# An FFT convolution's start-up: order of the first loads, two weight jobs ahead, 20 fillers

## The chip, the cores and the metric

The kernel runs on one core of a Trainium2 chip. A core has a matrix engine (TensorE, PE in the profile; its weight loads are listed as PEld), a vector engine (VectorE, DVE), an activation engine (ScalarE, ACT), a general engine (GpSimd, POOL) and a sequencer that issues transfers (SyncE, SP). Transfers are carried by 16 DMA engines. The metric is device time in microseconds for one execution; the kernel before takes 270.54 us, the median of three runs (270.21 to 270.58).

## The reference

A 7x7 convolution over a 224 x 224 picture with 96 channels in and 96 out, computed through Fourier transforms, so that both picture directions wrap around:

```python
wp = jnp.pad(w, ((0, H - K), (0, W - K), (0, 0), (0, 0)))
Xf = rfft2(x.astype(float32), axes=(1, 2))          # x: 1 x 224 x 224 x 96, bf16
Wf = rfft2(wp.astype(float32), axes=(0, 1))         # w: 7 x 7 x 96 x 96, bf16
Yf = jnp.einsum('bhwi,hwio->bhwo', Xf, Wf)
y = irfft2(Yf, s=(H, W), axes=(1, 2)).astype(bfloat16)
```

Because of the wrap-around, the first output columns need the last six columns of the picture, and the first rows need its last six rows.

## The kernel before, in words

The kernel does not transform the whole picture. It cuts the height into 8 blocks of 28 rows (with 6 rows of overlap, 34 in all), transforms each block along the height with a small matrix `Fm` (17 complex frequencies, held as real numbers), convolves along the width directly with 7 taps at each frequency, and transforms back with a small matrix `Gm`. The width is cut into 7 tiles of 32 columns. Products with a complex number are done with three real ones, and pairs of neighbouring columns are combined so that fewer products are needed; the combined planes are called `J`, and DVE computes them from the transformed pixels `xf`.

The weights need a transform of their own. `w` is loaded into `wq`, and a matrix `Em`, which stands behind it in the same buffer, turns it into the 50 planes of `WF`. This is done in groups of frequencies (`PGRP`): `prep_jobs(0)` covers frequencies 0 and 1, `prep_jobs(1)` frequencies 2 to 4, and so on. A group has 12 jobs, each of four TensorE products into one PSUM bank and a cast of that bank into `WF`; groups after the first end with three more jobs, subtractions on DVE (`diff`, WF from WF), which need all casts of their group.

Casts out of PSUM go through `evac`. It keeps a running cost for DVE and ACT in `load` and gives each cast to the engine whose cost is lower, as the program is written out, not as it runs. Each engine then works strictly in the order of the program text. There are eight PSUM banks, taken in turn; a product waits until the bank it takes has been cast.

What concerns the start, in the order of the program:

- SP issues the loads, lines 178 to 189. First come the wrap-around pixels, that is the last six columns (`xh_bufs`, two halves of the height with two transfers each: 112 rows and 6 rows, 1152 bytes a row), then the first half of the first tile's pixels (`load_x(0, 0)`, 112 rows and 6 rows of 6144 bytes), then the weights in five chunks, each in two transfers (2 partitions and 96), then the second half of the first tile's pixels, which waits for the third chunk of weights.
- Each of SP's transfers uses one of eight completion counters in turn. A transfer waits, before it is issued, until the transfer eight places ahead of it has landed.
- TensorE runs products on zeros (`warm`, tile `wu`): 17 at the very start, and 22 (line 707) between the products of the first pixels and those of the weights. All products of the weights wait for all five chunks.
- TensorE then transforms the wrap-around pixels (`a_bank`), the first half's pixels in three parts by frequency (`f_jobs`), runs the 22 fillers, the 12 jobs of the first weight group (48 products, line 709), and the second half's first part (line 711, 32 products).
- DVE makes the first planes `J` (line 715, `jit(0, 0)`), while POOL is still computing the matrix `Gm` (`build_g`, line 290) from a long chain of small operations; ACT takes its sine (`g_fin`, line 717, tile `ct` in the profile) and POOL forms the product (`Gm`).
- Then come the rounds (`b_round`), one for each frequency. Round 0 computes products from `xf` into one bank (copied by ACT to `tt_`), then `mid` jobs, products from `J` into a second bank, the sum `yf` on DVE, and `end` jobs. The second weight group's jobs are spread over `mid` and `end` of round 0 by `pace` (lines 744 and 745): 8 of its 15 jobs in `mid`, 7 in `end`.

From the third tile on the same rounds go on, with the transform of the next tile and the inverse transform of the tile before filled in between.

Of the kernel before, what the change touches and what calls it, by code (L numbers as in the profile page):

```python
# [32 lines left out]
PGRP = ((0, 2), (2, 5), (5, 8), (8, 11), (11, 14), (14, 17))  # L33
# [18 lines left out]
def slot(s, part):  # L52
    return part if s == 0 else 2 + 3 * (s - 1) + part
# [3 lines left out]
def kernel(  # L57
# [7 lines left out]
    _, H, W, C = x.shape  # L65
# [40 lines left out]
    def bank():  # L106
        return pools["psb"].tile([128, 512], F32, name="pb")

    load = {"v": 0.0, "a": 0.0}
# [3 lines left out]
    def apart(key, zone, r):  # L113
        for z, q in parts.setdefault(key, []):
            if z != zone and q.engine != r.ins.engine:
                tc.declare_no_dep(r.ins, q, reason="disjoint parts of one tile")
        parts[key].append((zone, r.ins))
        return r

    def evac(out_ap, in_ap, n):  # L120
        if tail[0]:
            return tail_evac(out_ap, in_ap, n)
        cv, ca = 180 + 1.0 * n, 160 + 0.85 * n
        if load["v"] + cv <= load["a"] + ca:
            load["v"] += cv
            return VE.tensor_copy(out=out_ap, in_=in_ap)
        load["a"] += ca
        return SE.copy(out=out_ap, in_=in_ap)
# [35 lines left out]
    def load_rows(xb, jg, w0, npx):  # L164
        h0 = jg * HB - PAD
        n = npx * C

        def ld(p0, p1, hh):
            return dma(xb[p0:p1, 0:n], x[0, hh:hh + (p1 - p0), w0:w0 + npx, :].rearrange("h w c -> h (w c)"))
        return ld(PAD, R, h0 + PAD), ld(0, PAD, h0 % H)  # L170

    def xbuf(t, jg):
        return (xn_bufs if t else x0_bufs)[jg]

    def load_x(t, jg):
        return load_rows(xbuf(t, jg), jg, t * 2 * TW, 2 * TW)

    wsrc = w.rearrange("kh kw i o -> (kh kw) (i o)")
    for jg in range(2):
        load_rows(xh_bufs[jg], jg, W - PAD, PAD)  # L180
    load_x(0, 0)
    wcut = [WC * c // NWC // 128 * 128 for c in range(NWC)] + [WC]
    wdma = []
    for c0, c1 in zip(wcut, wcut[1:]):
# [10 lines left out]
    def warm(n):  # L195
        pwu = bank()
        for _ in range(n):
            TE.matmul(pwu[:].rearrange("p (a b) -> p a b", a=4), lhsT=wu[:, 0:128], rhs=wur, start=True, stop=True)
# [141 lines left out]
    def prep_jobs(gi):  # L340
        s0, s1 = PGRP[gi]
        ns = s1 - s0
        full = gi == 0
        ncol = (NSLOT_OF(s0, s1) if full else 2 * ns) * NTAP
        nb = C // NB
        hb = NB // 2
        assert NB * ncol <= 512 and C2 % hb == 0

        def mk_(ob):
            def f():  # L350
                pw = bank()
                pv_ = pw[:, 0:NB * ncol].rearrange("p (k h q) -> p k h q", h=2, q=ncol)
                ev = Em[:, :, slot(s0, 0):slot(s1 - 1, 2) + 1, :]
                ev = ev.rearrange("p h a t -> p h (a t)") if full else ev.rearrange("p h (s r) t -> p h s (r t)", r=3)[:, :, :, 0:2 * NTAP]
                for k in range(hb):
                    o = ob * hb + k
                    TE.matmul(pv_[:, k], lhsT=wqx[0:PW2, o:o + 127 * C + 1:C], rhs=ev, start=True, stop=True)
                pv_ = pv_[0:C]
                o0, o1 = ob * hb, (ob + 1) * hb
                wv = WF[0:C, slot(s0, 0):slot(s1 - 1, 2) + 1]  # L360
                if full:
                    wv = wv.rearrange("i a t (h o) -> i (a t) h o", h=2)
                    apart(("W", gi), ob, evac(wv[..., o0:o1], pv_.rearrange("i k h q -> i q h k"), NB * ncol))
                    return
                wv = wv.rearrange("i (s r) t (h o) -> i s (r t) h o", r=3, h=2)
                apart(("W", gi), ob, evac(wv[:, :, 0:2 * NTAP, :, o0:o1],
                      pv_.rearrange("i k h (s q) -> i s q h k", s=ns), NB * ncol))
            return f

        def diff(s):  # L370
            def f():
                load["v"] += 60 + C * NTAP / 1.92
                w0, w1, w2 = (WF[0:C, slot(s, r)].rearrange("i t o -> i (t o)") for r in range(3))
                VE.tensor_tensor(out=w2, in0=w0, in1=w1, op=ALU.subtract)
            return f
        return [mk_(ob) for ob in range(nb)] + ([] if full else [diff(s) for s in range(s0, s1) if s not in REAL])

    def NSLOT_OF(s0, s1):
        return slot(s1 - 1, 2) + 1 - slot(s0, 0)
# [324 lines left out]
    for p in range(3):  # L704
        for f in fj[p][0]:
            f()
    for n in (11, 11):
        warm(n)
    for f in prep_jobs(0):
        f()  # L710
    last = [f() for f in fj[0][1]]
    for jg in range(2):
        for d in load_x(1, jg):
            tc.add_manual_dep(d.ins, last[0].ins.name, SYNC, reason="second tile's pixels later")
# [26 lines left out]
    def add(a, b, jobs):  # L741
        qs.append([a, b, jobs, len(jobs)])

    for gi in range(1, len(PGRP)):
        add(2 * PGRP[gi - 1][0], 2 * PGRP[gi - 1][1] - (2 if gi == 1 else 1), prep_jobs(gi))
    for t in range(2):
        scr_tiles[t] = dr_pool.tile([TW, NJ, NS, 4 * C], BF16, name="scr")
    bursts = {}
# [163 lines left out]
```

## Time and profile before

| | |
|---|---|
| median of three runs | 270.54 us (270.21 to 270.58) |
| profiled execution | 270.74 us, span of its instructions 269.0 us |
| granted TensorE clock | 0.997 |
| busy: PE, PEld | 257.9 us, 237.1 us |
| busy: DVE, ACT, POOL | 214.3 us, 195.5 us, 99.4 us |
| chain that ended last | PE 64%, DMA 12%, DVE 11%, ACT 7% |

The profile is one execution. Its span runs from the first to the last instruction; the time of the execution has 1.74 us more around it. A row of the timeline gives start, duration, engine, operation, tiles written and read, the size, how many instructions the row holds, and in brackets how long the engine had been idle and what ended that. A row of the chain gives the start, the length and the work that all later work waited for. A row of the windows gives, for a stretch of time, the busy time of each engine and the number of its instructions, then the granted clock, the share of time that the 16 DMA engines were busy, and GB/s. All kernel lines are recorded as one line (L89), that of a helper, so rows are told apart by their tiles.

### The profile page before, as it was taken

To read this page: it belongs to the slowest core of one execution; us is meant where nothing else is said; L and a number is where in the kernel's file an instruction comes from. 1 tells how busy PE (TensorE), PEld (TensorE's weight loads), DVE (VectorE), ACT (ScalarE), POOL (GpSimd) and SP (SyncE) were. 2 spreads that over 40 slices of the span, in tenths; PEclk is the share of its full clock that TensorE was granted. 3 is DMA by queue.
4 is the path that set the end of the run, shared out by engine and by line. 5 is a ranking of instruction groups with operands and counts; after the bars stand their busy time and mean duration, and the time that the engine had idled before them with its cause. 6 is when DMAs were issued, how large, how long until landed. Compare 5 with 4: busy or idle time off the path is not lost.

```text
span 269.0 us, 12171 instructions
## 1 busy us (share of the span) xinstructions
PE 257.9 (96%) x5144; PEld 237.1 (88%) x5144; DVE 214.3 (80%) x457; ACT 195.5 (73%) x483; POOL 99.4 (37%) x156
## 2 busy tenths in 40 slices
PE   8899999999999999999999999999998999899993
PEld 3679999999998999999999998989997989779862
DVE  5649998889899788778787888777887889778724
ACT  5549988587974578988988789886986864467113
POOL 7782315363647435322322222234132242522100
PEclk9999999999999999999999999999999999999998
DMA  6948011811111597987976486989658834888866
GB/s 171 230 129 217 6 46 46 243 47 67 46 46 50 163 276 135 294 249 206 289 207 198 133 246 192 250 223 332 224 151 152 255 98 154 198 231 212 223 118 205
DMA packets 47014, 46.78 MB, mean 174 GB/s; under 512 B 35286, under 2 KB 37986, under 8 KB 46960
## 3 DMA queue, kind: packets, MB, share of 16 engines
q1 hardware_dynamic: 44672, 43.94, 59.2%
q10 hardware_dynamic: 2288, 2.06, 2.8%
q8 instruction: 40, 0.66, 1.1%
q14 instruction: 14, 0.11, 0.1%
HBM read 24.65 MB, written 21.33 MB: 171 GB/s over the span
## 4 chain that ended last, share of the span: by engine, by line
PE 64%; DMA 12%; DVE 11%; ACT 7%; issue 3%; SPq 2%; DVEq 0%; ACTq 0%
PE pb L89 64%; DMA tt<-scr 5%; DMA wq<-in_w_dram 5%; DVE J L89 4%; ACT WF L89 3%; ACT xf L89 2%; DVE v L89 2%; DVE WF L89 2%; SPq L89 2%; DMA xf<-scrb 2%; DVE u L89 1%; DMA scrb<-yf 1%; DVE yf L89 1%; DVE xf L89 0%; DVE tt L89 0%
## 5 line engine op out<-in xcount | busy, mean ns | idle before, releaser
L89 PE MATMUL pb<-WF,J 96*128 96x96 bf16 x2821 | 162.6, 206 | 1.1 <-DVE J L89 0.9
L89 PEld LDWEIGHTS <-J 96*128 96x128 bf16 x2821 | 138.0, 98 | 10.5 <-issue 2.2
L89 POOL TENSOR_TENSOR yf<-v,u 128x384 bf16<-128x384 f32 x79 | 81.4, 1042 | 147.3 <-issue 86.9
L89 ACT CAST xf<-pb 96x408 bf16<-96x408 f32 (+3 forms) x145 | 67.8, 490 | 8.9 <-PE pb L89 5.3
L89 PE MATMUL pb<-WF,xf 96*128 96x96 bf16 x952 | 59.9, 206 | 0.5 <-ACT xf L89 0.5
L89 DVE TENSOR_TENSOR J<-xf 96x1824 bf16<-96x1824 bf16 (+1 forms) x84 | 56.9, 716 | 0.1
L89 PEld LDWEIGHTS <-xf 96*128 96x128 bf16 x952 | 47.0, 98 | 0.7 <-ACT xf L89 0.6
L89 PE MATMUL pb<-Fm,xn 118*128 118x136 bf16 (+3 forms) x640 | 45.5, 199 | 0.2 <-DVE u L89 0.2
L89 PE MATMUL pb<-tt,Gm 102*84 102x384 bf16 (+1 forms) x132 | 32.7, 327 | 2.4 <-DMA tt<-scr 2.3
L89 ACT CAST WF<-pb 96x480 bf16<-96x480 f32 (+1 forms) x59 | 29.1, 577 | 5.3 <-PE pb L89 5.3
L89 PEld LDWEIGHTS <-xn 118*128 118x128 bf16 x640 | 30.3, 97 | 0.3 <-issue 0.3
L89 ACT CAST J<-pb 84x384 bf16<-84x384 f32 (+1 forms) x64 | 27.6, 488 | 2.3 <-PE pb L89 2.0
L89 ACT CAST yo<-pb 84x384 bf16<-84x384 f32 (+1 forms) x63 | 26.9, 482 | 2.7 <-PE pb L89 2.7
L89 DVE TENSOR_TENSOR J<-J 96x912 bf16<-96x912 bf16 (+2 forms) x42 | 24.2, 576 | 0.0
L89 PE MATMUL pb<-wq 98*128 98x120 bf16 (+1 forms) x288 | 21.3, 226 | 0.3 <-DMA wq<-in_w_dram 0.3
L89 PEld LDWEIGHTS <-wq 98*128 98x128 bf16 x288 | 19.5, 151 | 0.8 <-issue 0.8
L89 PE MATMUL pb<-wu 128*128 128x512 bf16 (+1 forms) x75 | 16.5, 382 | 1.1 <-DVE ct L89 1.1
L89 PEld LDWEIGHTS <-wu 128*128 128x128 bf16 (+1 forms) x75 | 8.8, 119 | 7.7 <-issue 2.4
L89 DVE TENSOR_TENSOR yf<-v,u 128x384 bf16<-128x384 f32 x26 | 14.9, 571 | 0.9
L89 PEld LDWEIGHTS <-Gm 102*84 102x84 bf16 (+1 forms) x132 | 11.0, 117 | 3.5 <-DMA tt<-scr 2.9
L89 ACT COPY xf<-xf 96x816 bf16<-96x816 bf16 (+3 forms) x20 | 11.3, 632 | 0.0
L89 DVE CAST WF<-pb 96x480 bf16<-96x480 f32 (+1 forms) x13 | 7.5, 611 | 4.7 <-PE pb L89 4.7
(386 smaller groups left out, 234.4 us busy)
## 6 DMA issues: line engine op xcount, KB each, us to landing
scr<-yf SPq DMA_DIRECT2D x30, 288.0 KB
xn<-in_x_dram SPq DMA_DIRECT2D x12, 672.0 KB
tt<-scr SPq DMA_DIRECT2D x24, 336.0 KB
out_dram<-yo SPq DMA_DIRECT2D x12, 252.0 KB
out_dram<-J SPq DMA_DIRECT2D x12, 252.0 KB
tt<-scr SPq DMA_DIRECT2D x6, 288.0 KB
WF<-in_x_dram SPq DMA_DIRECT2D x2, 672.0 KB
out_dram<-tt SPq DMA_DIRECT2D x8, 168.0 KB
```

Of the source, the lines that this page charges most:

```text
L89: r = fn(*a, **k)
```

## The change

Three edits, all in the start:

1. `load_x(0, 0)` is issued ahead of the wrap-around pixels instead of behind them. The ten weight transfers stay behind both.
2. The first two jobs of the second weight group are written out right behind the first tile's second half (after line 711), ahead of `jit(0, 0)`, of `g_fin` and of round 0. Before them `load["v"]` is raised by a million, so that both casts go to ACT; the costs are reset a few lines on, as before. The other 13 jobs of that group are spread over round 0: 7 in `mid`, 6 in `end`.
3. The fillers are 10 + 10 instead of 11 + 11.

```diff
     wsrc = w.rearrange("kh kw i o -> (kh kw) (i o)")
+    load_x(0, 0)
     for jg in range(2):
         load_rows(xh_bufs[jg], jg, W - PAD, PAD)
-    load_x(0, 0)
...
-    for n in (11, 11):
+    for n in (10, 10):
         warm(n)
     for f in prep_jobs(0):
         f()
     last = [f() for f in fj[0][1]]
+    early = prep_jobs(1)
+    load["v"] += 1e6
+    for _ in range(2):
+        early.pop(0)()
...
     for gi in range(1, len(PGRP)):
-        add(2 * PGRP[gi - 1][0], 2 * PGRP[gi - 1][1] - (2 if gi == 1 else 1), prep_jobs(gi))
+        add(2 * PGRP[gi - 1][0], 2 * PGRP[gi - 1][1] - (2 if gi == 1 else 1), prep_jobs(gi) if gi > 1 else early)
```

Since `evac` counts costs as the text is written out, some later casts change their engine too: two go from DVE to ACT and one from ACT to DVE in round 0, and 11 between 183 and 217 us of the profile before (six from ACT to DVE, five from DVE to ACT).

## The prediction

> **What bounds the kernel now.** I read the busy shares and slices first, then the chain of waits, then the timeline of each engine for the first 45 us, where all three parts of the change lie, and last the DMA share by window.
>
> ```profile
> PE 257.9 (96%) x5144; PEld 237.1 (88%) x5144; DVE 214.3 (80%) x457; ACT 195.5 (73%) x483; POOL 99.4 (37%) x156
> ```
>
> TensorE is the busiest engine, but that is a mean. The chain, followed from the start to 50 us, says what each stage waits for:
>
> ```profile
> 9.55 6.52 DMA wq<-in_w_dram
> 16.07 0.14 issue
> 16.21 0.69 PE pb L89 x8
> ...
> 19.68 1.03 ACT xf L89 x2
> ...
> 21.63 4.19 ACT WF L89 x9
> ...
> 33.36 0.32 ACT tt__905 L89
> ...
> 41.53 1.75 DVE J L89 x2
> 43.28 0.28 DVE u L89
> ```
>
> The weight transfer sets the end of the first 16 us. From 16.9 to 33.7 us the chain lies on ACT, from 33.8 to 43.6 on DVE, and only then on TensorE (products, 64% of the whole chain). So the stage that the change touches is bounded by transfers, then by ACT, and TensorE has room in it. The rows of that stage:
>
> ```profile
> 10.98 4.91 PE L89 MATMUL pb<-wu 128*128 128x512 bf16 x22
> 16.21 3.15 PE L89 MATMUL pb<-wq 98*128 98x100 bf16 x48 [0.32 <-DMA wq<-in_w_dram]
> 20.76 0.51 PE L89 MATMUL pb<-WF,xf 96*128 96x96 bf16 x8 [0.46 <-ACT xf L89]
> 19.63 1.07 ACT L89 CAST xf<-pb 96x512 bf16<-96x512 f32 x2
> 20.89 0.37 ACT L89 ACTIVATE ct<-ct,ct 102x84 f32<-102x84 f32 x1 [0.19 <-POOL ct L89]
> 21.31 0.32 ACT L89 COPY tt__556<-pb 128x192 f32<-128x192 f32 x1
> 21.57 4.25 ACT L89 CAST WF<-pb 96x480 bf16<-96x480 f32 x9
> 21.27 1.10 DVE L89 TENSOR_TENSOR J<-xf 96x1824 bf16<-96x1824 bf16 x1
> 20.50 0.36 POOL L89 TENSOR_TENSOR ct<-ct,ct 102x84 f32<-102x84 f32 x1
> 21.34 1.27 POOL L89 TENSOR_TENSOR Gm<-ct,ct 102x84 bf16<-102x84 f32 x1 [0.48 <-ACT ct L89]
> ```
>
> The reader is to see three things: the products of the weights start when the transfer lands; TensorE waits about half a microsecond at 20.2 for ACT; and ACT itself waits at 20.70 for POOL's chain of small operations (the inverse matrix), which ends at 20.86 whatever the other engines do.
>
> **The change part by part.** Call d the time by which the weight products start earlier than 16.21.
>
> *Pixels first.* SP issues six pixel transfers from 0.80 to 3.06, then ten of weights. Bytes and issues are the same; only the order differs. The share of the 16 DMA engines at the start:
>
> ```profile
> 1.80:2.50 0.70, 0.70 (x3) 0.30 (x2) 0.53 (x4) 0.69 (x3) 0.62 (x3) 1.00 0.75 191
> 2.50:3.50 1.00, 1.00 (x4) 0.30 (x2) 0.93 (x5) 1.00 (x1) 0.73 (x5) 1.00 0.72 158
> 3.50:4.50 1.00, 1.00 (x4) 0.36 (x3) 0.40 (x2) 0.98 (x2) 0.85 (x5) 1.00 0.88 195
> ```
>
> (The last two columns are DMA share and GB/s.) Unused: 0.25 x 0.70 + 0.28 x 1.00 + 0.12 x 1.00 = 0.58 us. From 4.5 to 13 us the share is 1.02 to 1.05, so nothing is lost later. Short wrap-around rows (1152 B) go out first, in four issues of about 0.38 us, and the DMA engines run dry between them. With the long rows (6144 B) first there is a queue from the first packet on, so up to 0.58 us of it comes back. The nearest rows bound it: above by 1.57 us, the time by which the long rows' issue moves (from 2.37 to 0.80, the fifth place to the first); below by a loss (second rival). I take 0.6, the idle time, since bytes and packets stay.
>
> Behind these issues stand the weights'. In the built program each of SP's transfers takes one of eight completion counters in turn and waits until the transfer eight before it has landed. So the second weight chunk waits for transfers one and two, now the long rows instead of the wrap-around rows. Today that chunk is issued at 4.15 to 5.20 and its slowest engine needs it at 9.53, when the first chunk has landed (the issue at 9.55 waits for just that). With the long rows landing some 1.5 us earlier than today (7.46 for the 112 rows, 8.15 for the six, when SP's issues at 7.48 and 8.17 are released), the issue comes at about 6.0 to 6.7, plus 1.0 us to the first packet (0.80 to 1.80 today) 7.7, against a need at about 8.9. It fits, by about 1.2 us. The second tile half's pixels (issued at 12.92, behind the third chunk) move with the weights. TensorE takes the wrap-around products first; they now land last, but POOL's padding at 7.46 to 7.77 holds the sixth of them in any case, so I cost that at nothing; without that cover it would be the lateness of the landing.
>
> *20 fillers.* 22 take 4.91 us, 0.22 each, so TensorE is free 0.44 earlier: the last product ends at 15.89 today, 15.45 then, which is 0.76 before 16.21 (0.9 if the next products enter the pipe before that end). Fillers do not bind at d = 0.6; they would if the weights came more than that earlier.
>
> *Two early jobs.* Eight products of 0.065 us (32 take 2.1) = 0.5 us move into TensorE's wait at 20.2, and their two casts go to ACT by force. TensorE is thus 0.5 us further on, but it is not the bound here: the next bank, ACT and DVE set the pace (gain 0 on the path; it shows as slack). SP's loads of the second tile (20.24) wait for a pixel cast that still precedes the early ones. What counts is ACT. Before: the last pixel cast starts 20.12, then ct at 20.89, the copy, nine weight casts (0.455 from start to start; the last starts at 25.21 and ends 25.82). After, from the pixel cast: 20.60 - d first early cast, 21.06 - d second, 21.51 - d ct, but not before 20.89; then copy after 0.27 (no wait for the products now), casts after 0.26 more, eight of them, the last ending at ct + 0.53 + 7 x 0.455 + 0.60 = ct + 4.32. DVE gets two of the twelve casts instead of three, so ACT does one more, 0.455, paid by its waits (0.19 for POOL, some 0.15 for the products) and by the room ahead of POOL. With d = 0.6, ct = 20.91 and the last cast ends at 25.23, 0.59 earlier; with larger d POOL's 20.86 holds it at 0.61. So **the gain is about d, and never over 0.61**.
>
> From 25.7 to 33.7 ACT runs back to back, DVE's weight differences wait for that last cast (25.85 after 25.82), and DVE waits 0.44 us for ACT at 33.77, then runs back to back to 43.55, where TensorE waits for it. So the shift is handed on to 43.6 in full. From there TensorE is the chain; all loads hang on work that shifts alike.
>
> *Evacuations that change engine later.* The planner's running costs shift, and 11 casts from 183 to 217 us change between ACT and DVE, six to DVE, five to ACT. At 183.4 DVE gets a pixel cast (0.35 from start to start); a product at 190.86 needs a bank that DVE's u frees at 190.69, 0.17 us of room, so 0.0 to 0.2 is lost there, and an extra cast at 201.4 falls into 0.9 us of idle DVE. Bounds: -0.2 to +0.4 in all; I take +0.1.
>
> Sum, against the profiled execution's 270.74 (span 269.0, 1.74 around it): -0.6 + 0.1 = -0.5, 270.24. That execution is 0.20 above the median of the three runs, so **270.05** in the median.
>
> **The rivals.**
>
> *POOL is blocked by DVE.* The same POOL shape, 102x84, takes 0.36 us at 20.50 and 1.27 at 21.34, the latter beside DVE's J operation, which runs 21.27 to 22.37: POOL ended 0.24 after it. J starts when the pixel casts end, 21.27 - d. If d is over 0.77, J begins before POOL's sum at 20.50; that sum then ends about 20.42 + 1.10 + 0.24 = 21.76 instead of 20.86; ACT's ct waits for it, the tt copy and eight casts are queued behind ct, DVE's weight differences wait for these casts, and the gain of 0.6 becomes a loss of 0.3: with the later casts 270.9. The Trainium skill, SBUF — State Buffer, section "Who interferes with whom", says that a tensor_tensor with both inputs in SBUF contends with GpSimd's reads, and that whichever is issued first holds the ports for the whole instruction. By that rule, too, an order with POOL first would only delay J, and the trace's 1.27 against 0.36 agrees. For it: the fillers let d reach 0.76 to 0.9. Against: the DMA's idle time gives 0.6. Chance 0.2.
>
> *The counters starve the DMA: slower.* If the long rows land no earlier than today (7.46, 8.15), the second chunk is issued at about 8.2 to 8.8 and its first packet comes at 9.2 to 9.8, at or after the need at 9.53; each later chunk is pushed likewise. From that point every microsecond counts in full: 0.3 to 0.8 late is 270.9 to 271.4; I put it at 271.2. For it: chunks are issued by landings already (SP waits for them at 7.48, 8.17, 9.55). Against: the margin of 1.2. Chance 0.1.
>
> *The weights come no earlier.* The slowest DMA engine may have no idle time to give. Then d is 0 to 0.4, ACT's hole pays for its extra cast, and the time is 270.2 to 270.65, middle 270.45. For it: the fast engines' idle time is a mean. Chance 0.17.
>
> **How the numbers follow.** Forecast case 0.53, POOL 0.2, no earlier 0.17, starved 0.1. A measurement of this kernel tells about 0.2% (0.54 us) from no change, so the bounds are 270.0 and 271.08. The forecast case alone spans 269.75 to 270.4 (d from 0.45 to 0.61, later casts -0.2 to +0.3); it lies below 270.0 when these casts cost 0.05 or less at full gain, about half of it: 0.29, and 0.03 from the POOL case should the block be shorter, 0.32. Slower: the starved case 0.08, half of the POOL case (with the room at 190.9 gone as well) 0.10, and 0.04 for collisions of later transfers, 0.22. The rest, 0.46, is within. The range 269.65 to 271.0 leaves out about a tenth on each side.
>
> **What the next profile would show.** Right: the weight products start near 15.6; ct follows two weight casts on ACT at 20.9; the tt copy after it; DVE's u that today starts at 33.77 stands near 33.2, TensorE's stretch from 43.60 near 43.0. DMA share near 1.0 from 1.8 on. Wrong: POOL's sum at 20.5 over 1 us long and ACT idle before ct (first rival); SP's weight issues later than today with a DMA share under 0.8 between 6 and 9 us (second); weight products at 16.1 (third). A new TensorE wait between 183 and 217 us would show the moved casts mis-sized.

## The result, and the profile after

The changed kernel takes 271.51 us (median of 22 executions, 270.08 to 275.6); the kernel before, run beside it, 270.56 us (22 executions). The ratio is 1.0046, 95% interval 1.0027 to 1.0065: slower by about 0.9 us, where 270.05 was forecast and 271.0 was the upper end of the range. The ratio leaves out executions over 1.5% above the fastest of their kernel (three of the changed kernel's 22); the medians are over all.

The profiled execution took 271.39 us (span 269.7, granted clock 0.999). It is close to the median. In 8 of the 22 executions the mean granted clock was 0.994 or less, and these average 273.9 us; the other 14 average 271.1. I call the former low-clock executions from here on, and the others executions at full clock.

The chain of waits of the changed kernel (start, length, work), at the places shown before:

```profile
11.56 4.71 DMA WF<-in_x_dram
16.27 1.66 PE pb L89 x24
...
19.71 1.03 ACT xf L89 x2
20.74 0.92 ACT WF L89 x2
21.66 0.26 ACT ct L89
...
22.13 3.68 ACT WF L89 x8
...
41.51 1.74 DVE J L89 x2
43.25 0.28 DVE u L89
```

The reader is to see that every milestone stands where it stood: the products of the weights start at 16.25 (16.21 before), and DVE's `u` still ends at 43.5. The chain names the second half's pixels, which SP issues at 11.56 (12.92 before), as what was waited for, and so does the row of TensorE further on. But the products read the weights, and the last part of these landed at 16.11 (16.07 before), 0.14 us ahead of the products in both profiles: the wait is still for the weights, and the pixels only landed close by.

The windows of the changed kernel at the start (columns as before; the last three are granted clock, DMA share and GB/s):

```profile
1.80:2.50 0.70, 0.70 (x3) 0.30 (x2) 0.53 (x4) 0.69 (x3) 0.62 (x3) 1.00 0.99 132
2.50:3.50 1.00, 1.00 (x4) 0.30 (x2) 0.93 (x5) 1.00 (x1) 0.73 (x5) 1.00 0.89 344
3.50:4.50 1.00, 1.00 (x4) 0.37 (x3) 0.40 (x2) 0.97 (x2) 0.85 (x5) 1.00 0.99 303
...
6.50:7.00 0.50, 0.50 (x4) 0.26 (x3) 0.00 (x0) 0.00 (x0) 0.33 (x2) 1.00 0.57 129
7.00:7.50 0.50, 0.50 (x6) 0.27 (x4) 0.00 (x0) 0.00 (x0) 0.42 (x3) 1.00 0.78 129
7.50:8.00 0.50, 0.50 (x11) 0.49 (x9) 0.43 (x2) 0.29 (x1) 0.50 (x10) 1.00 0.56 93
```

The idle share of 1.8 to 4.5 us did fill up: 0.13 us are left of the 0.58. But a new hole opened from 6.5 to 8.0 us, where the share had been 1.02 to 1.03; there 0.5 x (0.43 + 0.22 + 0.44) = 0.55 us went. From 6 to 9 us as a whole, before and then after:

```profile
6.00:9.00 3.00, 2.26 (x40) 1.65 (x39) 1.41 (x3) 1.27 (x3) 2.63 (x15) 1.00 1.02 230
6.00:9.00 3.00, 3.00 (x50) 2.20 (x49) 1.43 (x3) 1.29 (x4) 2.61 (x15) 1.00 0.79 202
```

The timeline rows of the changed kernel around the early jobs, TensorE first:

```profile
10.96 4.48 PE L89 MATMUL pb<-wu 128*128 128x512 bf16 x20
16.25 3.14 PE L89 MATMUL pb<-wq 98*128 98x100 bf16 x48 [0.81 <-DMA WF<-in_x_dram]
20.16 0.71 PE L89 MATMUL pb<-wq 98*128 98x120 bf16 x8
20.64 1.01 ACT L89 CAST WF<-pb 96x480 bf16<-96x480 f32 x2
21.55 0.37 ACT L89 ACTIVATE ct<-ct,ct 102x84 f32<-102x84 f32 x1
21.82 0.31 ACT L89 COPY tt__566<-pb 128x192 f32<-128x192 f32 x1
22.02 3.78 ACT L89 CAST WF<-pb 96x480 bf16<-96x480 f32 x8
20.41 0.37 POOL L89 TENSOR_TENSOR ct<-ct,ct 102x84 f32<-102x84 f32 x1
```

The early products fill TensorE's old wait at 20.2, the two casts stand ahead of `ct`, eight casts follow, and POOL's sum takes 0.37 us, not blocked. TensorE's idle time ahead of the weight products grew from 0.32 to 0.81 us: the fillers end 0.45 earlier and the weights do not.

Late in the span the changed kernel has one wait that the kernel before lacks, and an older one behind it. First the rows of before, then those of the changed kernel:

```profile
190.52 0.50 PE L89 MATMUL pb<-WF,xf 96*128 96x96 bf16 x8
190.86 0.34 PE L89 MATMUL pb<-Fm,xn 118*128 118x136 bf16 x3
...
203.79 0.52 PE L89 MATMUL pb<-tt,Gm 102*84 102x384 bf16 x2 [1.10 <-DMA tt<-scr]
```

```profile
190.57 0.50 PE L89 MATMUL pb<-WF,xf 96*128 96x96 bf16 x8
191.14 0.34 PE L89 MATMUL pb<-Fm,xn 118*128 118x136 bf16 x3
...
203.86 0.52 PE L89 MATMUL pb<-tt,Gm 102*84 102x384 bf16 x2 [0.91 <-DMA tt<-scr]
```

From 190.57 to 191.14 are 0.57 us for eight products that took 0.34 before (190.52 to 190.86): 0.23 lost. At 203.86 TensorE waits for the read-back of the scratch rows (`tt` from `scr`: the sums `yf` are written to `scr` in DRAM and read back in another order), as it did before (1.10 us, to 203.79).

### The profile page after: what moved, and what is told of

It is laid out like the page before. It is cut to its first block, busy times and chain, and to the rows that moved or that the text cites. A ratio compares the mean times of both kernels' runs of the same rounds, so it can differ in the third digit from the quotient of the medians.

```text
span 269.7 us, 12165 instructions
## 1 busy us (share of the span) xinstructions
PE 258.1 (96%) x5142; PEld 237.2 (88%) x5142; DVE 213.9 (79%) x457; ACT 195.4 (72%) x483; POOL 98.6 (37%) x156
## 4 chain that ended last, share of the span: by engine, by line
PE 61%; DMA 15%; DVE 12%; ACT 6%; issue 2%; SPq 1%; DVEq 0%; ACTq 0%
PE pb L89 61%; DMA tt<-scr 5%; DVE J L89 4%; DMA WF<-in_x_dram 3%; DMA scrb<-yf 3%; ACT WF L89 3%; DVE WF L89 3%; DVE v L89 2%; ACT xf L89 2%; DMA wq<-in_w_dram 2%; DMA xf<-scrb 2%; DVE u L89 1%; SPq L89 1%; DVE yf L89 1%; DVE xf L89 0%
## 5 line engine op out<-in xcount | busy, mean ns | idle before, releaser
L89 ACT CAST WF<-pb 96x480 bf16<-96x480 f32 (+1 forms) x60 | 29.8, 581 | 5.4 <-PE pb L89 5.4
L89 DVE TENSOR_TENSOR yf<-v,u 128x384 bf16<-128x384 f32 x26 | 15.2, 584 | 0.9
L89 DVE CAST WF<-pb 96x400 bf16<-96x400 f32 (+1 forms) x12 | 6.9, 608 | 4.8 <-PE pb L89 4.8
```

What stands on the lines that cost most here:

```text
L89: r = fn(*a, **k)
```

## The experiments

Each run has 12 executions of its kernel, with 23 or 35 of the kernel before on the same chip. The table gives them together: the ratio, the number of low-clock executions, and the mean of the other executions less that of the kernel before (its own low-clock executions left out; 7 of 163 over the five chips). With some ten executions such a mean is good to about 0.5 us, an estimate from the scatter of the executions.

| kernel | ratio, interval | low-clock | others, us |
|---|---|---|---|
| e1 pixels first | 0.9991 [0.9964, 1.0018] | 1 | -0.2 |
| e2 early jobs | 1.0001 [0.9976, 1.0026] | 0 | +0.1 |
| e3 20 fillers | 1.0002 [0.9978, 1.0025] | 0 | +0.2 |
| e4 changed, 22 fillers | 0.9995 [0.9970, 1.0021] | 1 | +0.2 |
| e5 changed, again | 1.0047 [1.0015, 1.0079] | 6 | +0.6 |
| e6 pixels first, 20 fillers | 1.0016 [0.9991, 1.0040] | 2 | +0.4 |
| e7 early jobs, 20 fillers | 1.0046 [1.0022, 1.0069] | 2 | +1.0 |
| e8 changed, 16 fillers | 1.0072 [1.0045, 1.0100] | 9 | +1.2 |
| e9 changed, 24 fillers | 1.0031 [1.0006, 1.0056] | 1 | +0.7 |
| e10 changed, late casts back | 1.0025 [1.0001, 1.0048] | 1 | +0.5 |
| e11 both mendings | 1.0020 [0.9991, 1.0048] | 2 | 0.0 |
| e12 early, 22 fillers, casts back | 1.0000 [0.9978, 1.0022] | 0 | -0.1 |
| e13 before, late casts moved | 1.0061 [1.0029, 1.0093] | 6 | +0.9 |
| e14 before, 16 fillers | 1.0055 [1.0029, 1.0080] | 4 | +1.1 |
| e15 early, 20 fillers, casts back | 1.0012 [0.9989, 1.0035] | 1 | +0.2 |
| e16 early jobs, 20 fillers, again | 1.0055 [1.0032, 1.0079] | 5 | +1.4 |
| e17 before, first three casts | 1.0057 [1.0038, 1.0076] | 2 | +1.4 |
| e18 before, last eight casts | 1.0024 [1.0003, 1.0046] | 1 | +0.6 |

e1 to e4 ran on one chip, e5 to e8 on a second, e9 to e12 on a third, e13 to e16 on a fourth, e17 and e18 on a fifth. One execution of e9 (319.46 us at a clock of 0.756) stands alone, is not counted among the low-clock ones, and is not explained.

The second table is read from the traces: when TensorE starts the products of the weights, and when it loads the weights of the n-th of the 5,069 products that are not on zeros (us).

| profile | weights | 500th | 3,800th | 4,000th | 4,200th | 5,000th | last |
|---|---|---|---|---|---|---|---|
| before | 16.21 | 34.05 | 187.91 | 198.23 | 209.43 | 250.64 | 264.27 |
| after | 16.25 | 34.06 | 187.96 | 198.50 | 209.51 | 250.69 | 264.94 |
| e1 | 16.73 | 34.53 | 188.36 | 198.69 | 209.02 | 249.72 | 263.21 |
| e3 | 15.58 | 33.75 | 187.62 | 197.95 | 208.57 | 249.36 | 263.07 |
| e12 | 15.71 | 33.46 | 187.40 | 197.72 | 208.64 | 249.68 | 264.06 |
| e5 | 16.70 | 35.57 | 189.54 | 200.08 | 210.56 | 251.55 | 266.17 |
| e13 | 15.85 | 33.71 | 187.60 | 198.32 | 210.13 | 251.39 | 265.73 |
| e17 | 15.93 | 33.74 | 187.58 | 198.30 | 211.59 | 252.80 | 266.74 |
| e18 | 16.07 | 33.89 | 187.71 | 198.04 | 208.49 | 249.68 | 264.02 |

### One part at a time (e1 to e4)

Three theories stood at first: A, the transfers (weights later); B, the fillers (a gap that takes the clock down); C, the late casts.

e1, the order of the loads alone:

```diff
+    load_x(0, 0)
     for jg in range(2):
         load_rows(xh_bufs[jg], jg, W - PAD, PAD)
-    load_x(0, 0)
```

> Of the three parts only the order of the pixel transfers is changed; 22 fillers, no early jobs. Theory A (the transfers: the second half's pixels are issued 1.4 us earlier, 11.56 instead of 12.92, run beside the last weights on the faster DMA engines, and the slowest engine's weights land no earlier): weight products start at 16.0 to 16.3, the time is 0 to 0.3 us off the kernel before if the slowest engine is the same, and 0.5 to 1 us more on chips where it is slower. Theory B (the fillers: two fewer leave TensorE idle 0.8 us instead of 0.3 ahead of the weights and the granted clock falls to half for some microseconds in part of the executions): no change in the time, mean granted clock as before, 0.995 or more. Theory C (the casts that changed engine late): no change, since no cast changes its engine here.

e2, the early jobs alone:

```diff
     last = [f() for f in fj[0][1]]
+    early = prep_jobs(1)
+    load["v"] += 1e6
+    for _ in range(2):
+        early.pop(0)()
```

> Only the two early jobs; transfers and 22 fillers as before. Theory A: no loss; the time is within 0.2 us of the kernel before. Theory B: no loss, clock as before. Theory C (11 casts change engine between 183 and 217 us, TensorE waits for DVE at 190.9 and the last tile's transfers come later): the whole loss of 0.9 to 1.2 us is here, 271.5.

e3, 20 fillers alone:

```diff
-    for n in (11, 11):
+    for n in (10, 10):
```

> Only 20 fillers instead of 22; all else as before. Theory A and theory C: no change (weights set the start: products at 16.2). Theory B: the loss of 0.9 to 1.2 us in the median is here, and executions with a longer time have a mean granted clock of 0.98 to 0.99, against 0.995 and more in the others.

e4, the changed kernel with 22 fillers:

```diff
-    for n in (10, 10):
+    for n in (11, 11):
```

> The changed kernel with its 22 fillers put back. Theory A: as slow as the changed kernel, 0.9 to 1.2 us over the kernel before. Theory B: the loss is gone, within 0.3 us of the kernel before. Theory C: as slow as the changed kernel.

Measured: 269.91, 270.22, 270.21 and 270.51 us against 270.03; none can be told from the kernel before. A had put the loss into e4, B into e3 and C into e2 and e4: all three missed. So no single part carries the loss on this chip, and by e4 the order and the early jobs together do not either. (e2 and e4 contain the late casts as well; I come back to that.) The table of products shows against what spread the forecast of 0.6 us was set: with the loads in the same order the weight products start anywhere from 15.4 (e16) to 16.2 us, so the 16.21 of the profile of before was itself a late one. With late weights the early jobs do little for TensorE: its 500th product stands 17.81 us behind the start in the changed kernel, 17.80 and 17.84 in e1 and before. With early weights they do what the prediction says: with the start at 15.6 to 15.7 us the last of ACT's nine or eight weight casts ended at 25.14 to 25.26 us with them (e2, e4, e7, e12, e15) and at 25.52 without them (e3, started at 15.58), where ACT stood 0.78 us ahead of `ct` for POOL.

### Pairs and a longer gap (e5 to e8)

Theory D put the loss on pixels first with 20 fillers, F on pixels first with early jobs, G on the chip. e5 is the changed kernel as it is.

> The changed kernel as it is, beside the kernel before on one chip. Three theories stand. D: the pixels first and the two fillers fewer together leave TensorE idle for 0.8 us ahead of the weight products, and in part of the executions its clock is then taken down for a while: the ratio is 1.002 to 1.007 again, with a tail of executions 2 to 4 us longer at a mean clock below 0.994. F: it is the pixels first together with the early jobs that brings the slow tail, whatever the fillers (the changed kernel with 22 fillers had one execution of 12 at a clock of 0.989): the same figures here. G: the loss seen beside the first comparison belonged to that chip and not to the order of the work: within 0.2% here, no tail.

e6, order and fillers without the early jobs:

```diff
+    load_x(0, 0)
...
-    load_x(0, 0)
...
-    for n in (11, 11):
+    for n in (10, 10):
```

> Pixels first and 20 fillers, the two jobs left where they were. D: as the changed kernel, 1.002 to 1.007 with the tail. F and G: within 0.2% of the kernel before, no execution with a clock below 0.994.

e7, early jobs and fillers with the old order:

```diff
-    for n in (11, 11):
+    for n in (10, 10):
...
+    early = prep_jobs(1)
+    load["v"] += 1e6
+    for _ in range(2):
+        early.pop(0)()
```

> The two early jobs and 20 fillers, the loads in the order of before. D: the weights land up to 0.6 us earlier against the fillers than with the pixels first, so little idle time ahead of the products and no tail: within 0.2%. F: within 0.2%, no tail. G: within 0.2%. A tail here would speak against all three and for the early jobs with few fillers.

e8, the changed kernel with 16 fillers:

```diff
-    for n in (10, 10):
+    for n in (8, 8):
```

> The changed kernel with 16 fillers in place of 20: some 1.7 us more of idle TensorE (four products of 0.43 us at full clock) ahead of the weight products. D: the tail grows: more executions below a clock of 0.994, median at least 0.3% above the changed kernel on this chip. F and G: as the changed kernel, within 0.2% of it.

Measured: 271.96, 270.79, 271.54 and 272.88 us against 270.51. G falls in its plain form, since e5 repeats the first ratio on another chip. D and F fall as told, because e7, without pixels first, is as slow as the changed kernel, and nearly all its executions are at full clock; so there is a loss that the clock does not carry. But the longer gap of e8 does what D says: 9 of 12 executions are low-clock. (A filler takes 0.22 us, 4.48 for 20, so four fewer leave 0.9 us more of idle time and not the 1.7 expected: 1.71 us in the profile of e8 against 0.81.) The profile of e5 happens to be a low-clock execution (272.41 us, clock 0.994) and shows where. TensorE's row ahead of the weights, and the windows behind it:

```profile
16.70 3.37 PE L89 MATMUL pb<-wq 98*128 98x100 bf16 x48 [1.26 <-DMA wq<-in_w_dram]
```

```profile
15.00:17.00 2.00, 0.74 (x8) 0.33 (x6) 0.00 (x0) 0.00 (x0) 1.68 (x8) 1.00 0.56 173
17.00:19.00 2.00, 2.00 (x36) 2.00 (x35) 1.84 (x4) 1.59 (x4) 1.70 (x5) 1.00 0.03 12
19.00:21.00 2.00, 2.00 (x35) 2.00 (x34) 1.38 (x4) 1.71 (x4) 1.52 (x4) 0.51 0.00 0
21.00:23.00 2.00, 2.00 (x35) 2.00 (x33) 1.73 (x3) 1.49 (x4) 0.00 (x0) 0.63 0.50 79
23.00:25.00 2.00, 2.00 (x41) 2.00 (x39) 1.83 (x4) 2.00 (x7) 0.38 (x1) 1.00 0.88 283
```

The granted clock (third column from the end) is full right behind the gap and falls to half from 19 us on: 2 x 2 x (0.49 + 0.37) = 3.44 us at half speed, 2.4 us after the gap has ended. The 500th product comes at 35.57 instead of 34.51 (the changed kernel's 34.06 and the start 0.45 later): about 1.05 us. In the profile of e10 a gap of 0.84 us did the same, in that of e8 one of 1.71; in those of the changed kernel (0.81), e1 (0.85) and e14 (1.22) nothing fell. So a gap of about a microsecond may or may not bring the fall.

The Trainium skill, TensorE: Matmul & The Clock Gate, section "Part 1: The HAM clock gate (the "warmup" mystery)", has the clock watched in free-running windows of 3413 ns and halved after at least one idle window of that length. The length of the fall agrees (3.4 us), and free-running windows would explain why the same gap falls once and not another time. The trigger does not agree: gaps of 0.84 and 1.26 us were enough here, with TensorE at work on both sides of them, far from an idle window, and the measurement decides.

### The gap and the late casts mended (e9 to e12)

Theory H: a gap halves the clock. Theory K: the eleven late casts that change engine carry the loss of the other executions. e9, 24 fillers:

```diff
-    for n in (10, 10):
+    for n in (12, 12):
```

> The changed kernel with 24 fillers in place of 20. Two theories, which may hold side by side. H: in the executions in which the weights land late TensorE stands over about a microsecond ahead of their products, and its clock is then halved for 3.4 us, which costs 1.7 us at most; it does so in a third to half of the executions with 20 fillers. Four fillers more end 0.86 us later and leave no such gap: no more executions at a mean clock of 0.994 or less than the kernel before has (0 to 1 of 12), the mean of all executions 0.4 to 0.8 us lower than the changed kernel's; where weights land early the fillers end up to 0.7 us behind them and cost that much in these executions. K: the executions at full clock are 0.4 us above before by the eleven late casts that the early jobs put on the other engine: that stays, 1.001 to 1.003.

e10, the planner's costs raised behind round 0 by what the early jobs took out, so that every later cast is on its old engine:

```diff
     for r in range(NS + LAG):
+        if r == 1:
+            load["v"] += 660.0
+            load["a"] += 568.0
```

> The changed kernel, the two counters of VectorE and ScalarE raised behind round 0 by the 660 and 568 that the early jobs took out of them: every later cast is on the engine that it had before. H: the executions at half clock stay, 3 to 6 of 12, and the mean over all stays 0.8 us or more above before. K: TensorE's wait at 190.9 us falls from 0.24 to about nothing, and the executions at full clock are within 0.2 us of before.

e11 has the edits of e9 and of e10.

> Both mendings: 24 fillers and the late casts as before. H and K together: no tail and within 0.2% of before, at best 0.3 us faster by what the early jobs gain at an equal start. If it is still 0.3 us or more slower with no execution at half clock, the early jobs or the order of the loads cost in a way that is not named yet.

e12, e2 with e10's lines:

```diff
+    early = prep_jobs(1)
+    load["v"] += 1e6
+    for _ in range(2):
+        early.pop(0)()
...
+        if r == 1:
+            load["v"] += 660.0
+            load["a"] += 568.0
```

> The two early jobs alone, 22 fillers, the loads in the order of before, the late casts as before. H: as few executions at half clock as before has. K: 0.2 to 0.5 us faster than before (the early jobs had TensorE 0.27 us further on at its 500th product at an equal start), with nothing given back at 191 us; the transfers of the output at 203 us may take up all of it, then 0.

Measured: 271.39, 270.99, 270.25 and 270.37 us against 270.25. Each mending alone leaves a loss, both together bring the median back to that of before: e11 and e9 differ in the late casts alone, and e11 is 0.7 us lower at full clock. By their ratios, though, e9, e10 and e11 (1.0031, 1.0025, 1.0020) can't be told apart. H's forecast for e9 held in the count (one low-clock execution); for e11 it did not quite (two), and for e10 it failed: with 20 fillers and the late casts back it has one low-clock execution, where 3 to 6 were forecast. e10 missed K's forecast too: 0.5 us above before at full clock is left. e12 shows what the early jobs are worth without their late casts: no measurable gain (1.0000). Its table row shows where such a lead goes: 0.59 us ahead at the 500th product (0.50 of it by the start of the weights in that execution) and 0.51 at the 3,800th, 0.21 ahead at the last.

### The late casts alone (e13, e15, e16), and a gap alone (e14)

e13, the kernel before with the planner's costs lowered, so that the same eleven casts move and nothing else does:

```diff
     for r in range(NS + LAG):
+        if r == 1:
+            load["v"] -= 660.0
+            load["a"] -= 568.0
```

> The kernel before with the two counters lowered by 660 and 568 behind round 0: the same eleven casts change their engine as in the changed kernel, and nothing else does. K (the late casts cost): TensorE is 0.2 us later at 191 to 203 us and the executions at full clock are 0.2 to 0.8 us above before. L (they cost nothing, and the early jobs or the order of the loads cost otherwise): within 0.2 us of before.

e14, the kernel before with 16 fillers:

```diff
-    for n in (11, 11):
+    for n in (8, 8):
```

> The kernel before with 16 fillers in place of 22: these end at 14.6 us where the weights land at 15.2 to 16.1, so TensorE stands 0.6 to 1.5 us. H (a gap halves the clock for a while): part of the executions, 3 to 9 of 12, at a mean clock of 0.994 or less and 1 to 1.7 us longer, none of the rest slower. Against H: all executions as before.

e15, e7 with the late casts put back:

```diff
     for r in range(NS + LAG):
+        if r == 1:
+            load["v"] += 660.0
+            load["a"] += 568.0
```

> Early jobs and 20 fillers, the loads in the order of before, with the late casts put back on the engine that they had before. K: 0.4 to 0.9 us below the same kernel without that, which runs beside it, and within 0.2% of before. L: as that kernel, about 1.0 us above before.

e16 is e7 once more.

> Early jobs and 20 fillers, the loads in the order of before, beside the kernel with the late casts put back. Its ratio was 1.0046 on another chip, nearly all at full clock. K and L: about 1.004 again. If it is within 0.2% of before here, the loss belonged to the executions or the chip of that comparison, and the late casts can't be blamed for it.

Measured: 271.93, 271.55, 270.60 and 271.98 us against 270.36. K stands and L falls: eleven casts moved in a kernel that is otherwise the old one cost 1.0061, as much as the whole change within the noise; put back in e15 they take 1.4 us off e16's median. Both sizes are above what K had forecast. What K had not said: half of e13's executions are low-clock, though its start is that of before. There is a second place where a gap in TensorE's work lets the clock fall: e14's profile shows it, and e17's below, in the wait for the scratch rows.

e14 is slower as H said (4 low-clock), but its gap of 1.22 us ahead of the weights did not bring the fall in the profiled execution; the fall came at 203 us. Its executions at full clock are 1.1 us above before too, which H does not explain.

The profile of e16 holds something else: the prediction's first rival, POOL blocked by DVE. Its weight products started at 15.36 us, 0.85 ahead of before, and so did DVE's `J`:

```profile
20.41 1.34 POOL L89 TENSOR_TENSOR ct<-ct,ct 102x84 f32<-102x84 f32 x1
20.41 1.51 DVE L89 TENSOR_TENSOR J<-xf 96x1824 bf16<-96x1824 bf16 x2
21.79 0.37 ACT L89 ACTIVATE ct<-ct,ct 102x84 f32<-102x84 f32 x1 [1.01 <-POOL ct L89]
```

POOL's sum took 1.34 us in place of 0.36 or 0.37 in all other profiles, and ended at 21.75, where the rival had put it (21.76). ACT's `ct` waited 1.01 us for it, the last of the casts behind it ended at 26.01 (25.14 in e7, the same kernel, started at 15.61), and the 500th product came at 34.24 (33.46 in e7): an earlier start cost 0.8 us. In e7 and e3, with `J` at 20.63 and 20.62, POOL's sum was first and took 0.36 and 0.37 us. With 22 fillers no profile starts before 15.7 us, since TensorE is at the fillers until then; with 20 the start can come at 15.36, with 16, which end at 14.6, as soon as the weights land (15.2 us at the earliest in the old order). So this block may be what 16 fillers cost at full clock; the one profile of e14 started at 15.79 and does not have it, so that is not shown.

The low-clock executions can be sorted by the two suspects. With late casts and 20 or 16 fillers 30 of 70 executions are low-clock (the changed kernel, e5, e7, e8, e16); with late casts and 22 or 24 fillers 8 of 47 (e2, e4, e9, e13); with 20 or 16 fillers and no late casts 8 of 60 (e3, e6, e10, e14, e15); with neither 3 of 36 (e1, e11, e12); e17 and e18, which move part of the casts, are left out. So they come mostly where both stand together; the groups are from different chips.

### Which of the eleven (e17, e18)

Both are the kernel before with the planner's costs untouched and single casts turned over to the other engine:

```diff
+FLIP = (278, 279, 280)
...
+        vec = load["v"] + cv <= load["a"] + ca
+        load["v" if vec else "a"] += cv if vec else ca
+        ncast[0] += 1
+        if ncast[0] in FLIP:
+            vec = not vec
+        return VE.tensor_copy(out=out_ap, in_=in_ap) if vec else SE.copy(out=out_ap, in_=in_ap)
```

These are the three at 183.4 to 183.8 us; e18 has the other eight, 196.3 to 217.1 us, in `FLIP`:

```diff
-FLIP = (278, 279, 280)
+FLIP = (298, 307, 309, 318, 320, 332, 333, 334)
```

> The kernel before with three casts alone on the other engine, those that started at 183.36, 183.62 and 183.84 us. M (these carry the cost: VectorE late, its sum late for TensorE at 190.9 us, the writes of the scratch rows late, and so the wait at 203 us longer): 0.4 to 0.9 us above before at full clock, some executions at half clock as with all eleven. N (the eight behind carry it): at most 0.2 us above before.

> The kernel before with the eight casts alone on the other engine that started between 196.29 and 217.05 us. M: within 0.2 us of before, no wait at 190.9 us. N: 0.4 to 0.9 us above before at full clock, some executions at half clock.

Measured: 271.79 and 270.72 us against 270.19. The three casts carry most of it (M), though with 1.4 us at full clock more than M's 0.4 to 0.9 and more than all eleven in e13 (0.9, on another chip); the eight perhaps 0.6 us, at the edge of what these runs tell and against M's 0.2. So the split is not exact. TensorE's waits in e17 (line 90 there is line 89 of the others), and then the one of e18:

```profile
190.94 0.34 PE L90 MATMUL pb<-Fm,xn 118*128 118x136 bf16 x3 [0.24 <-DVE u L90]
204.35 0.86 PE L90 MATMUL pb<-tt,Gm 102*84 102x384 bf16 x2 [1.60 <-DMA tt<-scr]
```

```profile
202.84 0.52 PE L90 MATMUL pb<-tt,Gm 102*84 102x384 bf16 x2 [0.35 <-DMA tt<-scr]
```

The windows of e17 behind its second wait:

```profile
202.00:204.00 2.00, 0.76 (x18) 0.61 (x15) 0.82 (x2) 0.78 (x2) 1.61 (x2) 1.00 1.33 172
204.00:206.00 2.00, 1.65 (x15) 1.36 (x16) 0.55 (x1) 0.47 (x1) 0.00 (x0) 0.59 0.68 103
206.00:208.00 2.00, 2.00 (x29) 2.00 (x27) 1.59 (x3) 0.49 (x1) 0.00 (x0) 0.56 0.66 153
208.00:210.00 2.00, 2.00 (x44) 1.89 (x41) 2.00 (x5) 1.86 (x5) 0.00 (x0) 1.00 1.00 246
```

Of e17's two waits one is for DVE's `u` (0.24 us) and one for the transfer (1.60 us), and then the clock is at half for 2 x 2 x (0.41 + 0.44) = 3.4 us. Here TensorE is the bound, so the fall counts in full: from the 4,000th to the 4,200th product e17 takes 13.29 us against 11.20 before, of which 0.5 is the longer wait and 1.6 the clock.

How the three casts get to the first wait shows in DVE's rows, of before and then of e13:

```profile
183.84 0.54 DVE L89 CAST yo<-pb 84x384 bf16<-84x384 f32 x1
...
190.34 0.34 DVE L89 SCALAR_TENSOR_TENSOR u<-pb,tt__5700 128x192 f32<-128x192 f32 x1
```

```profile
183.53 0.43 DVE L89 CAST xf<-pb 96x272 bf16<-96x272 f32 x1
183.88 0.54 DVE L89 CAST yo<-pb 84x384 bf16<-84x384 f32 x1
...
190.56 0.34 DVE L89 SCALAR_TENSOR_TENSOR u<-pb,tt__5700 128x192 f32<-128x192 f32 x1
```

One more cast (183.53) in a DVE that has little room from there to 190.9. TensorE's 3,800th product is 0.31 earlier than in the profile of before, yet `u` is 0.22 later. The sums `yf` are late alike, and SP issues the write of the scratch rows that stood 0.94 us behind the 3,800th product in before, e15 and e18 (0.95 there) at 1.28 to 1.47 behind it in after, e13, e16 and e17.

The second wait is longer as well. TensorE goes on 16.07 us behind the 3,800th product in the mean of the ten profiles with the three casts moved (15.33 to 16.89), 15.49 in that of the ten without (15.00 to 16.32): 0.6 us, and a longer gap ahead of it. The chain of waits names the transfer, here in before and in e13:

```profile
198.20 5.54 DMA tt<-scr
```

```profile
197.90 6.55 DMA tt<-scr
```

It is the first of seven reads of the scratch rows, and TensorE goes on 0.04 to 0.06 us behind the landing of its last part in all twenty profiles. But SP issues it 10.28 to 10.31 us behind the 3,800th product in all twenty: it is not issued later with the casts moved, it takes longer. Nor can the late write above hold it up directly, since the DMA engines are almost idle in between: from 6 to 9 us behind that product their share is 0.01 in e18 and 0.25, the highest, in e15. What does differ right ahead of the read is a write of the output (`out_dram` from `J`): issued at 8.99 to 9.01 and landed at 11.55 to 11.60 us behind the product in the ten profiles without the moved casts, issued at 9.23 to 9.41 and landed at 12.12 to 12.57 in the ten with them. Fifteen of the read's sixteen parts land alike in the two groups (the fifteenth 15.04 us behind the product in the mean with the moved casts, 14.98 without); it is the last part alone that is late. That the output write, closer ahead of the read, holds up that part fits these figures; no run moves it alone, so it is not shown.

## Why the prediction was wrong

**What bounds the kernel** was read rightly for the first 45 us: transfers, ACT, DVE, then TensorE, in the same order after the change.

**Pixels first: the step failed.** The idle DMA time of 1.8 to 4.5 us was used, as said, but it did not become an earlier landing; 0.55 us was lost again between 6.5 and 8.0. The step that failed is the margin of 1.2 us on the second chunk. Its issue was forecast for 6.0 to 6.7 us and ran from 5.51 to 6.52, but its need had been put at 8.9, from the landing of the first chunk, which is the landing of its slowest part. From 6.5 us on the share was 0.57: part of the engines had by then done with that chunk and stood idle. So the rival of the counters was at work in part, with its sign in the profile (0.79 of DMA share between 6 and 9 us), though not by the cause that it gave, since the long rows landed at 5.49 and 5.93 us, 2.0 and 2.2 earlier than before (1.5 was forecast). The rival "the weights come no earlier" described the outcome: 16.25. Over all profiles the last of the sixteen parts of the last weight chunk landed at 15.55 us in the mean of eleven executions with the old order (15.21 to 16.07) and at 15.99 in the mean of nine with pixels first (14.96 to 16.59): 0.4 us later, not 0.6 earlier. The last part trails the one before it by 0.8 us in the mean with pixels first, by 0.3 with the old order. The Trainium skill, DMA: Bandwidth & Descriptors, section "Why a DMA increments its semaphore by 16 and not by 1", has a rule by which a transfer of 2 or 6 rows is carried by that many engines, the lowest-numbered ones. If so, these have more to carry than the rest, which fits one late part; no run here names its engine.

**20 fillers: costed at nothing, true by itself and not with late weights.** They ended at 15.44 as reckoned (15.45). What the working lacked is a price for a gap: it treated an idle TensorE as free. e5's profile puts 1.05 us on a gap of 1.26 where the clock falls, and with 16 fillers 9 of 12 executions of the changed kernel are low-clock. (Without the late casts fewer fillers alone seldom do it, 8 of 60.)

**Two early jobs: the mechanism as told, the handing-on not.** Casts, `ct`, the sum on POOL and the eight casts came in the order described; at d = 0 the last cast ended at 25.80 (25.82 before), the case "ACT's hole pays for its extra cast". The rival with the blocked POOL did not come about in this profile (0.37 us), but it was rightly reckoned: in e16, at d = 0.85, it is there as forecast (POOL's sum ended at 21.75 us against 21.76), and the last cast is 0.19 us behind that of before, where a loss of 0.3 was forecast. But "handed on to 43.6 in full, from there TensorE is the chain" was wrong behind 43.6: what is gained reaches the 3,800th product and then meets the wait at 203 us, whose end hangs on transfers. The profile of e12 is 0.51 us ahead at that product and 0.21 at the last, and e12's ratio is 1.0000. So even a d of 0.6 would most likely not have been worth 0.6.

**The late casts: the term that was mis-sized, and the largest.** Forecast +0.1 us, -0.2 to +0.4. The 0.0 to 0.2 at 190.9 us was nearly right (0.23, 0.24). The rest was costed by cover: room on DVE at 201 us, nothing said of the transfers behind the casts. By themselves the eleven cost 0.9 us at full clock (e13) and 1.0061 with the low-clock executions; moving them back takes 1.4 us off e16's median. The forecast's condition "a new TensorE wait between 183 and 217 us would show the moved casts mis-sized" is what the profile has at 190.9.

So the loss of the changed kernel has two causes that the runs show, and one that may join them. The late casts cost most: put into the old kernel they bring the loss (e13), taken out of e16 they end it within the noise (e15). Their way goes over DVE at 183 us to TensorE's wait at 190.9, and a longer read at 203 us goes with them; how they lengthen it is argued only. The longer gaps, ahead of the weights and at 203 us, let the clock fall in part of the executions, mostly where late casts and fewer fillers stand together. And where weights land early with 20 fillers or fewer, `J` can block POOL (e16); how often is not known. The parts do not add up exactly: e10, with the casts back, is still 0.5 us above before at full clock, and e9, with 24 fillers, 0.7; only both mendings together (e11) bring the median back to 270.25. None of the eighteen is faster than the kernel before beyond its interval. Open are what makes the last part of the read at 203 us late, why the late casts cost nothing in e2 and e4 (the same casts on the chip of e1 to e4, with the same late write of the output), and why 16 fillers cost a microsecond in executions without a fall.

## What to carry to other kernels

Where engines are chosen by running costs as the program is written out, an edit at the start moves work at the end: list what moved, follow each moved cast to the transfers that hang on it, or set the costs back behind the edit (two lines here). Take a transfer's need from when most of its parts are done and its landing from the slowest one. And look at several executions of a start-up: in the one profile of before the last weights landed 0.5 us behind the mean of the old order, and that was the very figure on which the forecast was built. A rival that does not come about in one execution can do so in the next: the start of e16 was 0.25 us earlier than that of e7, and POOL was blocked.

## What the runs showed of the hardware

- A gap of about a microsecond in TensorE's work can halve its granted clock for 3.4 us, from the end of the gap (e17) or up to 2.5 us behind it (e10): 0.84 us in e10, 1.26 in e5, 1.71 in e8, 1.50 at 203 us in e14 and 1.60 there in e17 did. Others of 0.81 to 1.71 us (0.81 in after, 1.22 in e14 ahead of the weights, 1.71 in e13 at 203 us) passed without it. Where TensorE is the bound a fall costs 1.6 us, at the start 1.05.
- Such falls are seen in the mean granted clock of an execution without a trace: the profiles with a fall ahead of the last 20 us show 0.989 to 0.994, those without 0.996 to 1.0.
- The landing of one and the same set of loads varies by 0.9 us between executions and chips (15.21 to 16.07 us in the old order, eleven profiles).
- A POOL sum of 102x84 takes 0.36 or 0.37 us alone and 1.34 beside a DVE operation that starts with it (e16); with POOL 0.14 and 0.20 us ahead (e7, e3) it took 0.36 and 0.37.
- The cost of the late casts differs: 0.9 to 1.4 us at full clock in e13, e16 and e17, and nothing measurable in e2 and e4 on another chip, whose waits at 203 us were 0.92 and 0.34 us.
